# The first stage of an attention-and-mixing kernel: its loads further ahead and in program order, and two steps of token mixing exchanged

## The chip, the cores and the metric

The kernel runs on one core of a Trainium2 chip. The metric is the device time of one execution in microseconds (us). Three timed runs of the kernel before took 830.56, 832.79 and 835.46 us; the median is 832.79.

The engines carry the names of the profile: PE multiplies matrices (PEld loads its weights), DVE is the vector engine, ACT the scalar engine, POOL the GpSimd engine, and SP issues the transfers from memory (DMA). Each engine works through its own instructions in a fixed order, and so does SP with the transfers that it issues: an instruction that waits holds up all that stand behind it on the same engine.

## The reference

Three blocks follow each other. All matrices are float32 and the weights of the second block come as 64-bit floats.

```python
# 1. attention: 4 images, 8 heads, 576 positions, head width 64
#    a) pooled: q, k, v averaged over groups of 4 positions (144 groups), softmax, times v; each result serves 4 positions
#    b) local: only positions nearer than 4 to each other, softmax, times v
out = repeat(softmax(qd @ kd.T / 8) @ vd, 4) + softmax(mask(q @ k.T / 8)) @ v
# 2. mixing, x of 4 x 576 x 512
h  = relu(x.T @ w_tok1) @ w_tok2            # token mixing, 576 -> 256 -> 576
u  = x + h.T
y  = u + relu(u @ w_ch1) @ w_ch2            # channel mixing, 512 -> 1536 -> 512
# 3. four causal attention experts of width 64 with a gate that keeps the best two
```

## The kernel before

The program has three stages. The first holds the attention and the token mixing, the second the channel mixing, the third the experts. The change touches the first stage only, so this section stays with it.

A **unit** is one image and one pair of heads: 16 units, numbered 0 to 15. A unit's data are the queries `qT` (288 KB), the keys `kz` (two transfers of 144 KB, one for each head, into a tile whose other half is zero), the values by windows `vz` (two transfers of 160 KB) and the values for pooling `vp` (288 KB): 1,184 KB in all. The tiles `kz`, `vz` and `qz` exist `KB` and `VB` times and are used in turn; `KB` and `VB` are 3, and `vp` has two buffers.

The stage is a software pipeline. **Step i** of its loop (lines 468 to 486) does, for different units:

- `load_qk` asks for the queries and keys of unit i+3 (`LA` + 1);
- `values(i)` multiplies the finished probabilities with the values on PE: `pod` for the pooled part, `ol` for the local one. DVE adds both into `u`, the result. After it the tile `vz` of unit i is free;
- `local(i+2)` and `pooled(i+2)`: POOL and DVE form the pooled queries `qz` and keys `kd` (line 295, a sum over `kz` on DVE), PE forms the scores `sl` and `sd`, DVE their maxima (`nmx`, `nd`), ACT the exponentials (10 for `P`, 3 for `Pd`), DVE the reciprocals of the sums (`rs`, `rd`), POOL multiplies (lines 324 and 345);
- `turns(i+1)` transposes `P` and `Pd` on PE (`tl`, `pdt`), and ACT copies them to `PT` and `PdT`;
- `tok_step`, for a whole pair of units: `tok_turn` transposes `u` on PE (`tx`) and splits it into a high part on ACT (`xh`) and a low part on DVE (`xl`); `tok_first` multiplies with the first weights (`h`); `tok_second` with the second (`pu`, 24 products), and DVE adds to `u` (line 433). In even steps there are `tok_turn(i-2)` and `tok_second(i-4)`, in odd steps `tok_first(i-3)`;
- up to four of the seven pieces of token-mixing weights (`wt`) and, from step 3 on, one piece of the channel-mixing weights (`wc`, 512 KB each) are loaded and **converted**: two passes on ACT (lines 190, 192), three on DVE (194 to 196), one on POOL (200), and a split into high and low on ACT and DVE (137, 147);
- `load_v` asks for the values of unit i+3 (`VB`).

What sets the order: PE takes its instructions in the order of the program (`behind` ties each to the one before). For the other engines, and for SP, a scheduler in the compiler chooses the order by its own estimate of times, and moves loads and conversions ahead of the place where the program has them. So the distance at which a load is issued is not simply `LA` or `VB`. Products go to four PSUM banks of one kind and two pairs of another: a product waits until the bank that it gets has been read.

Of the kernel before, what the change touches and what calls it, by code (L numbers as in the profile page):

```python
# [7 lines left out]
F32 = mybir.dt.float32  # L8
# [8 lines left out]
B, H, S, D = 4, 8, 576, 64  # L17
# [9 lines left out]
PK, PQ = SD // 2, 2 * SD // 3  # L27
# [18 lines left out]
ZENG = ['any', 'any']  # L46
PRE = False
ABANKS, CBANKS = (4, 2), (6, 1)
START = 'q0 q1 v0 q2 v1 v2'
XLO = 'gpsimd'  # L50
CONV0 = 3
UB = 5
TAIL = [1, 1, 1, 1]
ULO = 'vector'
LA = 2
WT = 4
VB = 3
KB = 3


@with_exitstack
def body(ctx, tc, qT, kT, vw, vp, wt1, wt2, wc1, wc2, wq, wk, wvg, wo, out):
    nc = tc.nc

    def pool(name, side=None, space=None, stack=ctx):
        kw = {"side": side} if side else {}
        if space is not None:
            kw["space"] = space
        return stack.enter_context(tc.tile_pool(name=name, bufs=1, reuse_waits="tile", **kw))
# [21 lines left out]
    order = {"on": True, "last": None}  # L91

    def behind(ins):

        if order["on"]:
            if order["last"] is not None:
                tc.add_manual_dep(ins.ins, order["last"].ins.name,
                                  mybir.DependencyInfo(mybir.DependencyClass.NoSync, mybir.DependencyReason.DATA),
                                  reason="order")
            order["last"] = ins  # L100

    def mm(*a, **kw):
        behind(nc.tensor.matmul(*a, **kw))  # L103

    def tp(*a):
        behind(nc.tensor.transpose(*a))
# [29 lines left out]
    def split(hi, lo, src, relu=False, scale=None):  # L136
        nc.scalar.activation(hi, src, AF.Relu if relu else AF.Copy, **({"scale": scale} if scale else {}))  # L137
        lowpart(lo, src, hi, relu, scale)
# [18 lines left out]
    def flat(t, shape):  # L157
        return t.rearrange("p c n -> p (c n)") if len(shape) == 3 else t

    def load_split(p, dram, shape, name, stage):  # L160
        raw = stage.tile(shape, F32, tag="raw", bufs=2, name=name + "_raw")
        nc.sync.dma_start(raw, dram)
        hi = p.tile(shape, F32R, name=name + "_hi")
        lo = p.tile(shape, F32R, name=name + "_lo")
        split(hi, lo, raw)
        return hi, lo

    def load_f32(dram, shape, name, dst=None):

        P0, n = shape[0], 1  # L170
        for d in shape[1:]:
            n *= d
        if dram.dtype == F32:
            if dst is None:
                dst = pv.tile(shape, F32, tag="w64t", bufs=2, name=name + "_t")
            nc.sync.dma_start(dst, dram)
            return dst
        raw = pv.tile([P0, n, 2], I32, tag="raw64", bufs=2, name=name + "_raw")
        d32 = dram.bitcast(I32)
        if len(shape) == 3:  # L180
            nc.sync.dma_start(raw.rearrange("p (c n) t -> p c (n t)", c=shape[1]), d32)
        else:
            nc.sync.dma_start(raw.rearrange("p n t -> p (n t)"), d32)
        h = raw[:, :, 1]
        a = pv.tile([P0, n], I32, tag="w64a", bufs=2, name=name + "_a")
        f = pv.tile([P0, n], I32, tag="w64f", bufs=2, name=name + "_f")
        g = pv.tile([P0, n], F32, tag="w64g", bufs=2, name=name + "_g")
        t = pv.tile([P0, n], F32, tag="w64t", bufs=2, name=name + "_t")

        nc.scalar.activation(t.bitcast(I32), raw.bitcast(U32)[:, :, 0], AF.Copy, scale=2.0 ** -29)  # L190

        nc.scalar.activation(g, h.bitcast(F32), AF.Abs)

        nc.vector.tensor_scalar(a, h, 3, 0x3FFFFFF8, op0=OP.logical_shift_left, op1=OP.bitwise_and)
        nc.vector.scalar_tensor_tensor(f, h, -0x40000000, a, op0=OP.bitwise_and, op1=OP.bitwise_or)
        nc.vector.scalar_tensor_tensor(f.bitcast(F32), g, 2.0 ** -15, f.bitcast(F32), op0=OP.is_ge, op1=OP.mult)
        if dst is None:
            dst = t.rearrange("p (c n) -> p c n", c=shape[1]) if len(shape) == 3 else t

        nc.gpsimd.tensor_tensor(flat(dst, shape).bitcast(I32), f, t.bitcast(I32), op=OP.add)  # L200
        return dst
# [12 lines left out]
    pa = pool("pa", stack=sA)  # L214
# [27 lines left out]

    KZ = [pa.tile([128, 2, S], F32, name=f"kz{i}") for i in range(KB)]
    VZ = [pa.tile([128, 2, NW, D], F32, name=f"vz{i}") for i in range(VB)]

    QZ = [pa.tile([128, 2, SD], F32, name=f"qz{i}") for i in range(KB)]

    def zero(tiles, i, eng):

        for h in range(2):  # L250
            eng.memset(tiles[i][64 * h:64 * h + 64, 1 - h], 0.0)

    Vl, Vd = {}, {}

    def load_v(b, p):
        i = b * NP + p
        if i < VB:
            zero(VZ, i, getattr(nc, ZENG[1]))
        Vl[b, p] = VZ[(b * NP + p) % VB]
        for h in range(2):  # L260
            nc.sync.dma_start(Vl[b, p][64 * h:64 * h + 64, h], vw[b, p, 64 * h:64 * h + 64])
        raw = pa.tile([PK, 4, 4, D], F32, tag="vp", bufs=2, name=f"vp{b}{p}")
        nc.sync.dma_start(raw, vp[b, p])
        vd = pa.tile([PK, 4, D], F32, tag="vd", bufs=3, name=f"vd{b}{p}")
        spare("v", i).tensor_tensor(raw[:, :, 0:2], raw[:, :, 0:2], raw[:, :, 2:4], op=OP.add)
        spare("w", i).tensor_tensor(vd, raw[:, :, 0], raw[:, :, 1], op=OP.add)
        Vd[b, p] = vd
# [1 line left out]
    QK = {}  # L269

    def load_qk(b, p):
        q = pa.tile([128, S], F32, tag="qT", bufs=3, name=f"qT{b}_{p}")
        nc.sync.dma_start(q, qT[b, p])
        i = b * NP + p
        if i < KB:
            zero(KZ, i, getattr(nc, ZENG[0]))
            zero(QZ, i, nc.gpsimd)
        kz = KZ[i % KB]
        for h in range(2):
            nc.sync.dma_start(kz[64 * h:64 * h + 64, h], kT[b, p, 64 * h:64 * h + 64])  # L280
        QK[b, p] = (q, kz, QZ[i % KB])

    SC = {}
# [151 lines left out]
    units = [(b, p) for b in range(B) for p in range(NP)]  # L435
    for what in START.split():
        (load_qk if what[0] == "q" else load_v)(*units[int(what[1])])

    n = len(units)
# [20 lines left out]

    def tok_step(i):

        for what, k in ((tok_turn, i - 2), (tok_first, i - 3), (tok_second, i - 4)):
            if k % 2 == 0 and 0 <= k < n:
                with ahead(what.__name__):
                    what(units[k][0], units[k][1] // 2)

    for i in range(n):
        if i + LA + 1 < n:
            load_qk(*units[i + LA + 1])  # L470
        values(*units[i])
# [7 lines left out]
        tok_step(i)  # L479
        for _ in range(WT):  # L480
            if tokw:
                tokw.pop(0)()
        if i >= CONV0 and conv[0][0] == 0:
            convert()
        if i + VB < n:
            load_v(*units[i + VB])
    order["on"] = False
    sA.close()


# [279 lines left out]
    for i, (b, p) in enumerate(pairs):  # L770
# [13 lines left out]
        last = nxt is None  # L784
# [80 lines left out]
```

## Time and profile before

| | |
|---|---|
| median of three runs | 832.79 us |
| the profiled execution | 831.15 us |
| its span, first to last instruction | 829.3 us |
| PE busy in the span | 696.0 us (84%) |
| DVE, ACT, POOL busy | 492.0, 392.2, 163.4 us |
| TensorE clock granted, mean | 0.925 of full speed |
| DMA over the span | 57 GB/s |

The profiled execution lies 1.64 us under the median of the runs, and its span 1.85 us under its own time. The first stage ends at 277.5 us, where PE begins its first product of the channel mixing; from there to 560 us PE is almost never idle. The first 235 us are where PE stands still for much of the time, and a row of the timeline there shows in square brackets how long an engine was idle before an instruction and what ended that idle time.

### The profile page before, as it was taken

The numbers are of one execution on the slowest core, as the hardware profiler recorded it, in microseconds if no ns is written. First come the engines' busy times: TensorE is split into PE (matmuls) and PEld (weight loads), VectorE is DVE, ScalarE is ACT, GpSimd is POOL, SyncE is SP. The second block draws the span as 40 slices with busy tenths as digits, with TensorE's granted clock in tenths as the row PEclk, the third lists the DMA queues.
The fourth block names the chain that finished last, engine by engine and source line by source line (L and its number), as shares of the span: only waits on it lengthen the run. The fifth ranks groups of instructions, "written<-read, shape, count | busy, mean of one in ns | idle before, by whom it ended". The sixth has DMA issues, their size and how long they took to land. (4 is left out here: it accounts for less than half of the span.)

```text
span 829.3 us, 15409 instructions
## 1 busy us (share of the span) xinstructions
PE 696.0 (84%) x5816; PEld 648.7 (78%) x5816; DVE 492.0 (59%) x1203; ACT 392.2 (47%) x1273; POOL 163.4 (20%) x183
## 2 busy tenths in 40 slices
PE   4424468568589999999999999999989989989994
PEld 3324368557578999999999999999987868779863
DVE  5598955334445479487558445644287556657760
ACT  6356653363365254354344223422266475566662
POOL 5575653333321012020011000000420010010000
PEclk8567598798799999999999999999999999999997
DMA  8545552252210022031011001000021031021111
GB/s 208 141 126 171 157 123 60 60 117 60 59 34 2 1 89 65 2 116 37 1 51 53 1 1 39 15 1 1 1 58 31 1 86 30 9 78 30 44 45 57
DMA packets 28578, 46.88 MB, mean 57 GB/s; under 512 B 3224, under 2 KB 16024, under 8 KB 28504
## 3 DMA queue, kind: packets, MB, share of 16 engines
q1 hardware_dynamic: 28504, 45.90, 20.7%
q8 instruction: 46, 0.75, 0.4%
q14 instruction: 28, 0.23, 0.1%
HBM read 36.45 MB, written 4.72 MB: 50 GB/s over the span
## 5 line engine op out<-in xcount | busy, mean ns | idle before, releaser
L103 PE MATMUL c<-ul,wch 128*128 128x288 f32 x384 | 113.7, 296 | 0.6 <-DVE ul L506 0.6
L103 PE MATMUL c<-uh,wch 128*128 128x288 f32 x384 | 113.6, 296 | 0.4 <-DVE acc L529 0.4
L103 PE MATMUL c<-hh,wch 128*128 128x288 f32 x384 | 113.8, 296 | 0.0
L103 PE MATMUL c<-hh,wcl 128*128 128x288 f32 x384 | 113.2, 295 | 0.0
L103 PE MATMUL c<-hl,wch 128*128 128x288 f32 x384 | 113.2, 295 | 0.0
L103 PE MATMUL c<-uh,wcl 128*128 128x288 f32 x384 | 113.2, 295 | 0.0
L137 ACT ACTIVATE hh<-c 128x288 fp32r<-128x288 f32 x96 | 39.1, 408 | 122.1 <-PE c L103 122.1
L143 DVE SCALAR_TENSOR_TENSOR hl<-c,hh 128x288 fp32r<-128x288 f32 x96 | 43.5, 453 | 64.6 <-ACT hh L137 64.6
L103 PEld LDWEIGHTS c<-ul,wch 128*128 128x128 f32 x384 | 72.4, 189 | 1.5 <-DVE ul L506 1.3
L103 PEld LDWEIGHTS c<-uh,wch 128*128 128x128 f32 x384 | 72.2, 188 | 0.9 <-DVE acc L529 0.9
L103 PEld LDWEIGHTS c<-hh,wch 128*128 128x128 f32 x384 | 72.2, 188 | 0.2
L103 PEld LDWEIGHTS c<-hl,wch 128*128 128x128 f32 x384 | 72.3, 188 | 0.0
L103 PEld LDWEIGHTS c<-hh,wcl 128*128 128x128 f32 x384 | 72.3, 188 | 0.0
L103 PEld LDWEIGHTS c<-uh,wcl 128*128 128x128 f32 x384 | 72.2, 188 | 0.0
L200 POOL TENSOR_TENSOR wc_t<-wc_f,wc_t 128x512 int32<-128x512 int32 x24 | 33.7, 1409 | 171.3 <-ACT wc_t L190 155.3
L505 ACT ACTIVATE uh<-u 128x288 fp32r<-128x288 f32 x128 | 52.9, 441 | 27.3 <-PE c L103 27.3
L506 DVE TENSOR_TENSOR ul<-u,uh 128x288 fp32r<-128x288 f32 x128 | 56.4, 470 | 8.8 <-ACT uh L505 8.7
L700 ACT ACTIVATE Pc<-s,nm 112x576 f32<-112x576 f32 (+4 forms) x80 | 44.3, 555 | 25.6 <-DVE nm L697 13.2
L103 PE MATMUL pod<-PdT,vd 72*64 72x144 f32 x128 | 13.4, 339 | 50.7 <-ACT PdT L363 45.7
L103 PE MATMUL pu<-wt_hi,h1h 128*128 128x288 f32 x64 | 24.0, 375 | 36.4 <-DVE xl L147 35.2
L319 ACT ACTIVATE P<-sl,nmx 128x64 f32<-128x64 f32 x160 | 48.6, 341 | 8.7 <-DVE nmx L313 8.6
L295 DVE TENSOR_REDUCE kd<-kz 128x144 f32<-128x1152 f32 x16 | 21.6, 1348 | 51.3 <-DMA kz<-in_kT_dram 51.3
(166 smaller groups left out, 1880.1 us busy)
## 6 DMA issues: line engine op xcount, KB each, us to landing
wc_raw<-in_wc_dram SPq DMA_DIRECT2D x24, 512.0 KB
vz<-in_vw_dram SPq DMA_DIRECT2D x32, 160.0 KB
qT<-in_qT_dram SPq DMA_DIRECT2D x16, 288.0 KB
kz<-in_kT_dram SPq DMA_DIRECT2D x32, 144.0 KB
vp<-in_vp_dram SPq DMA_DIRECT2D x16, 288.0 KB
K<-K SPq DMA_DIRECT2D x64, 72.0 KB
out_dram<-y SPq DMA_DIRECT2D x16, 232.0 KB
wt_raw<-in_wt_dram SPq DMA_DIRECT2D x4, 288.0 KB
```

What stands on the lines that cost most here:

```text
L103: behind(nc.tensor.matmul(*a, **kw))
L137: nc.scalar.activation(hi, src, AF.Relu if relu else AF.Copy, **({"scale": scale} if scale else {}))
L143: nc.vector.scalar_tensor_tensor(lo, src, 0.0, h, op0=OP.max, op1=OP.subtract)
L200: nc.gpsimd.tensor_tensor(flat(dst, shape).bitcast(I32), f, t.bitcast(I32), op=OP.add)
L295: nc.vector.tensor_reduce(kd, kz.rearrange("p h (g r) -> p g h r", r=4), axis=AX.XY, op=OP.add)
L319: nc.scalar.activation(P[:, t, h], sv[:, bk, i], AF.Exp, bias=nmx[:, bk, i:i + 1], scale=0.125, accum_out=sm[:, t, h:h + 1])
L505: nc.scalar.activation(hi, u, AF.Copy)
L506: getattr(nc, ULO).tensor_tensor(lo, u, hi.bitcast(F32), op=OP.subtract)
L700: nc.scalar.activation(pv_, sv, AF.Exp, bias=nm[:nq], accum_out=su[:nq])
```

## The change

Six things are edited. `KB` and `VB` go from 3 to 4 and `vp` gets a third buffer (`vd` a fourth), so that `load_qk` asks for unit i+4 and `load_v` for unit i+4. The list of first loads `START` holds four units. All loads of the first stage go through a new helper `fetch`, which ties each load to the load before it, so that SP issues them in the order of the program, weights included. At most three pieces of `wt` go into a step. In `tok_step` the second product of token mixing now stands before the turning. The scratch memory that the compiler reserves for DMA descriptors is cut from 16 KB to 1 KB in each partition, which makes room for the larger tiles.

```diff
-START = 'q0 q1 v0 q2 v1 v2'
+START = 'q0 q1 v0 q2 v1 q3 v2 v3'
-LA = 2
-WT = 4
-VB = 3
-KB = 3
+LA = 3
+WT = 3
+VB = 4
+KB = 4
...
+    queue = {"on": True, "last": None}
+
+    def fetch(dst, src):
+
+        ins = nc.sync.dma_start(dst, src)
+        if queue["on"]:
+            if queue["last"] is not None:
+                tc.add_manual_dep(ins.ins, queue["last"].ins.name,
+                                  mybir.DependencyInfo(mybir.DependencyClass.NoSync, mybir.DependencyReason.DATA),
+                                  reason="queue")
+            queue["last"] = ins
...
-            nc.sync.dma_start(Vl[b, p][64 * h:64 * h + 64, h], vw[b, p, 64 * h:64 * h + 64])
-        raw = pa.tile([PK, 4, 4, D], F32, tag="vp", bufs=2, name=f"vp{b}{p}")
-        nc.sync.dma_start(raw, vp[b, p])
-        vd = pa.tile([PK, 4, D], F32, tag="vd", bufs=3, name=f"vd{b}{p}")
+            fetch(Vl[b, p][64 * h:64 * h + 64, h], vw[b, p, 64 * h:64 * h + 64])
+        raw = pa.tile([PK, 4, 4, D], F32, tag="vp", bufs=3, name=f"vp{b}{p}")
+        fetch(raw, vp[b, p])
+        vd = pa.tile([PK, 4, D], F32, tag="vd", bufs=VB, name=f"vd{b}{p}")
...
-        for what, k in ((tok_turn, i - 2), (tok_first, i - 3), (tok_second, i - 4)):
+        for what, k in ((tok_second, i - 4), (tok_turn, i - 2), (tok_first, i - 3)):
...
-    order["on"] = False
+    order["on"] = queue["on"] = False
...
-    nc = bacc.Bacc("TRN2", target_bir_lowering=False, num_devices=1)
+    nc = bacc.Bacc("TRN2", target_bir_lowering=False, num_devices=1, dynamic_dma_scratch_size=1024)
```

The other loads of the stage (`qT`, `kz`, `wt`, `wc`) change from `nc.sync.dma_start` to `fetch` in the same way.

**SP, the loads that are issued during step 6.** Before (`vp23` is unit 11, `vz0` will hold unit 9, `qT2_3` and `kz2` are unit 11):

```order
L263 DMA vp23_1878<-in_vp_dram 72x1024
L261 DMA vz0_111<-in_vw_dram 64x640 x2
L273 DMA qT2_3_1693<-in_qT_dram 128x576
L280 DMA kz2_110<-in_kT_dram 64x576 x2
L263 DMA vp30_2032<-in_vp_dram 72x1024
```

Now (`vz2` and `vp22` are unit 10, `qT2_3` and `kz3` unit 11, `wc2_1` a piece of the channel-mixing weights; all rows have the line of `fetch`):

```order
L106 DMA vz2_114<-in_vw_dram 64x640 x2
L106 DMA vp22_1540<-in_vp_dram 72x1024
L106 DMA qT2_3_1545<-in_qT_dram 128x576
L106 DMA kz3_111<-in_kT_dram 64x576 x2
L106 DMA wc2_1_raw_1692<-in_wc2_dram 128x1024
L106 DMA vz3_115<-in_vw_dram 64x640 x2
```

`vz` now leads the group in place of `vp`, the keys are those of the same unit 11 in both, and one piece of `wc` stands behind the keys of steps 2 to 8, where before all those pieces had been asked for by step 4.

**PE, step 6, from the turns of unit 7 to the values of unit 7.** Before:

```order
L106 MATMUL tx0_1447<-ident_58,u1_90 116x128 x4
L106 MATMUL tx1_1456<-ident_58,u1_90 116x128 x4
L106 MATMUL tx2_1465<-ident_58,u1_90 112x128 x2
L103 MATMUL pu_1472<-wt2_00_hi_475,h1h_1310 128x288
...
L103 MATMUL pu_1496<-wt2_11_hi_642,h1l_1311 128x288
L103 MATMUL pod_1529<-PdT_1438,vd13_1164 64x144 x4
```

Now:

```order
L118 MATMUL pdt_1459<-ident_58,Pd_1271 72x96 x6
L115 MATMUL pu_1467<-wt2_00_hi_614,h1h_1330 128x288
...
L115 MATMUL pu_1491<-wt2_11_hi_806,h1l_1331 128x288
L118 MATMUL tx0_1499<-ident_58,u1_90 116x128 x4
L118 MATMUL tx1_1508<-ident_58,u1_90 116x128 x4
L118 MATMUL tx2_1517<-ident_58,u1_90 112x128 x2
L115 MATMUL pod_1549<-PdT_1458,vd13_994 64x144 x4
```

The 24 products `pu` moved from behind the turning `tx` to ahead of it.

**DVE, the same step.** Before (`kd` is the pooled key of unit 11, `xl` the low part of the turned `u`, `rs` belongs to the softmax of unit 8):

```order
L295 TENSOR_REDUCE kd_1922<-kz2_110 128x144
L147 TENSOR_TENSOR xl_1453<-tx0_1447,xh_1452 116x512
L147 TENSOR_TENSOR xl_1462<-tx1_1456,xh_1461 116x512
L147 TENSOR_TENSOR xl_1469<-tx2_1465,xh_1468 112x256
L322 TENSOR_SCALAR rs_1408<-sm_1397 128x10
L323 RECIPROCAL rs_1408<-rs_1408 128x10
L433 TENSOR_TENSOR u0_89<-pu_1472,u0_89 128x288
```

Now:

```order
L445 TENSOR_TENSOR u0_89<-pu_1467,u0_89 128x288
L307 TENSOR_REDUCE kd_1942<-kz3_111 128x144
L445 TENSOR_TENSOR u0_89<-pu_1475,u0_89 128x288
L445 TENSOR_TENSOR u0_89<-pu_1483,u0_89 128x288
L206 TENSOR_SCALAR wc2_1_a_1694<-wc2_1_raw_1692 128x512
L445 TENSOR_TENSOR u0_89<-pu_1491,u0_89 128x288
L334 TENSOR_SCALAR rs_1428<-sm_1417 128x10
...
L159 TENSOR_TENSOR xl_1505<-tx0_1499,xh_1504 116x512
```

The sum `kd` of unit 11 still stands in step 6, now between the additions of token mixing; the first pass over a piece of `wc` stands ahead of `rs`, and `xl` comes last.

## Rows read from the trace of the kernel before

**Rows 1.** Busy time by stretch, cut at the starts of steps 0, 2, 5, 9, 12.
```profile
core 0: us, PE busy (x) PEld busy (x) DVE busy (x) ACT busy (x) POOL busy (x), PEclk, DMA share, GB/s
0.00:35.30 35.30, 10.85 (x81) 8.39 (x81) 16.37 (x32) 17.62 (x67) 17.40 (x41) 0.72 0.71 184
35.30:76.80 41.50, 15.21 (x188) 13.91 (x188) 37.51 (x55) 20.58 (x78) 27.45 (x27) 0.66 0.47 141
76.80:131.90 55.10, 34.29 (x355) 31.83 (x355) 42.48 (x72) 31.04 (x121) 31.41 (x30) 0.72 0.47 124
131.90:194.10 62.20, 40.90 (x503) 38.74 (x502) 25.10 (x60) 25.94 (x128) 22.45 (x28) 0.84 0.37 79
194.10:235.00 40.90, 29.40 (x375) 27.51 (x374) 16.22 (x40) 18.68 (x95) 12.90 (x16) 0.87 0.31 69
```

**Rows 2.** Waits from 131.86 to 235 us: total us, times, longest.
```profile
DVE kd L295 <- DMA kz<-in_kT_dram: 42.3, 6, 8.9
PE pu L103 <- DVE xl L147: 28.2, 3, 9.6
```

**Rows 3.** Timeline of SP in step 6: start, us, load issued.
```profile
146.75 0.33 SPq L263 DMA_DIRECT2D vp<-in_vp_dram  x1
...
149.00 1.10 SPq L280 DMA_DIRECT2D kz<-in_kT_dram  x2
```

**Rows 4.** Waits of SP over the whole span: total us, times, longest.
```profile
SPq L263 <- POOL vd L266: 89.5, 10, 14.5
```

**Rows 5.** Timeline of PE, steps 6 to 13; in brackets idle before and releaser.
```profile
141.85 0.71 PE L103 MATMUL pod<-PdT,vd 72*64 72x144 f32 x8 [1.13 <-ACT PdT L363]
142.40 1.33 PE L103 MATMUL ol<-PT,vz 128*64 128x58 f32 x40
...
157.83 0.61 PE L103 MATMUL pu<-wt_hi,h1h 128*128 128x288 f32 x1 [9.63 <-DVE xl L147]
...
163.10 0.71 PE L103 MATMUL pod<-PdT,vd 72*64 72x144 f32 x8
...
173.09 0.71 PE L103 MATMUL pod<-PdT,vd 72*64 72x144 f32 x8 [1.12 <-ACT PdT L363]
...
248.63 0.71 PE L103 MATMUL pod<-PdT,vd 72*64 72x144 f32 x8
```

**Rows 6.** Timeline of DVE in step 6, same columns.
```profile
155.83 1.35 DVE L295 TENSOR_REDUCE kd<-kz 128x144 f32<-128x1152 f32 x1 [8.92 <-DMA kz<-in_kT_dram]
157.10 1.61 DVE L147 TENSOR_TENSOR xl<-tx,xh 116x512 fp32r<-116x512 f32 x3
```

**Rows 7.** Groups of instructions to 268 us: busy us, mean ns, idle before.
```profile
L340 ACT ACTIVATE Pd<-sd,nd 96x144 f32<-96x144 f32 x48 | 18.1, 417 | 0.0
L147 DVE TENSOR_TENSOR xl<-tx,xh 116x512 fp32r<-116x512 f32 x14 | 9.1, 681 | 5.2 <-ACT xh L137 5.2
L137 ACT ACTIVATE xh<-tx 116x512 fp32r<-116x512 f32 x14 | 8.8, 634 | 0.0
L192 ACT ACTIVATE wc_g<-wc_raw 128x512 f32<-128x512 f32 x10 | 6.7, 685 | 9.3 <-DMA wc_raw<-in_wc_dram 9.3
```

**Rows 8.** Timeline of DVE before step 3: a key tile lands, pieces of `wc` land.
```profile
21.07 1.35 DVE L295 TENSOR_REDUCE kd<-kz 128x144 f32<-128x1152 f32 x1 [3.08 <-DMA kz<-in_kT_dram]
...
63.99 0.43 DVE L194 TENSOR_SCALAR wc_a<-wc_raw 128x512 int32<-128x512 int32 x1 [1.69 <-DMA wc_raw<-in_wc_dram]
...
66.86 0.43 DVE L194 TENSOR_SCALAR wc_a<-wc_raw 128x512 int32<-128x512 int32 x1 [0.32 <-DMA wc_raw<-in_wc_dram]
...
70.34 1.97 DVE L194 TENSOR_SCALAR wc_a<-wc_raw 128x512 int32<-128x512 int32 x1
```

**Rows 9.** Timeline of ACT before step 0.
```profile
33.47 0.67 ACT L190 ACTIVATE wt_t<-wt_raw 116x512 int32<-116x512 uint32 x1 [3.15 <-DMA wt_raw<-in_wt_dram]
...
34.59 0.63 ACT L363 ACTIVATE PdT<-pdt 72x576 f32<-72x576 f32 x1
```

**Rows 10.** Timeline of POOL, step 1.
```profile
69.10 2.93 POOL L200 TENSOR_TENSOR wc_t<-wc_f,wc_t 128x512 int32<-128x512 int32 x2
```

More of the change, by code (lines that the diff above doesn't have):

```diff
@@ L161, in load_split @@
         raw = stage.tile(shape, F32, tag="raw", bufs=2, name=name + "_raw")
-        nc.sync.dma_start(raw, dram)
+        fetch(raw, dram)
         hi = p.tile(shape, F32R, name=name + "_hi")
@@ L175, in load_f32 @@
                 dst = pv.tile(shape, F32, tag="w64t", bufs=2, name=name + "_t")
-            nc.sync.dma_start(dst, dram)
+            fetch(dst, dram)
             return dst
@@ L180, in load_f32 @@
         if len(shape) == 3:
-            nc.sync.dma_start(raw.rearrange("p (c n) t -> p c (n t)", c=shape[1]), d32)
+            fetch(raw.rearrange("p (c n) t -> p c (n t)", c=shape[1]), d32)
         else:
-            nc.sync.dma_start(raw.rearrange("p n t -> p (n t)"), d32)
+            fetch(raw.rearrange("p n t -> p (n t)"), d32)
         h = raw[:, :, 1]
@@ L271, in load_qk @@
     def load_qk(b, p):
-        q = pa.tile([128, S], F32, tag="qT", bufs=3, name=f"qT{b}_{p}")
-        nc.sync.dma_start(q, qT[b, p])
+        q = pa.tile([128, S], F32, tag="qT", bufs=KB, name=f"qT{b}_{p}")
+        fetch(q, qT[b, p])
         i = b * NP + p
@@ L279, in load_qk @@
         for h in range(2):
-            nc.sync.dma_start(kz[64 * h:64 * h + 64, h], kT[b, p, 64 * h:64 * h + 64])
+            fetch(kz[64 * h:64 * h + 64, h], kT[b, p, 64 * h:64 * h + 64])
         QK[b, p] = (q, kz, QZ[i % KB])
```

## Prediction

> **What bounds the kernel now.** I read the busy time by stretch first. PE is the engine with most to do, and the reader is to see where it stands still: in the five stretches up to 235 us it is busy for 130.7 us of 235 [rows 1]. No other engine is full there, except DVE between 35 and 77 us (37.5 of 41.5 us). So the first stage is bound by waits, and the list of waits comes next. From step 5 to step 12 two of them lead: DVE waits 42.3 us for keys, and PE waits 28.2 us, three times, until DVE has formed `xl` [rows 2]. The third view, the timeline of step 6, shows that these two are one chain. The step starts at 141.85 us (its `pod`), and its products with `vz` end at 143.73, 1.9 us later. SP issues the next group of loads only at 146.75, 4.9 us after the start, because `vp` leads the group and waits for a buffer that POOL frees with `vd` [rows 3, 4]. The keys, last in the group, are there at 155.83, 9.1 us after the first issue. DVE stands at `kd` until then; behind it come the three `xl`, and only the first of them frees the bank in which the products `pu` may begin, at 157.83 [rows 5, 6]. The 24 `pu` take until 163.1, and the step has lasted 21.25 us. The odd step behind it, which has neither `tx` nor `pu`, lasts 10.0 (163.10 to 173.09). All of the time from step 5 to 12 is pairs of this kind.
>
> **The change, part by part.** The sum is made in lengths of steps, against the profiled execution (831.15 us, 1.64 under the median).
>
> *Even steps without a weight (10).* SP's group is led by `vz` now, which waits only for the products of the step: first issue 2.0 us after the start in place of 4.9. The group is as large as before (1,184 KB), so I take the same 9.1 us: keys at 11.1, `kd` done at 12.4. The products `pu` no longer wait for `xl`; they run under the wait for the keys, 5.3 us that leave the chain. What is late next is the bank of `tx`: by the new order the second addition of token mixing, which frees it, stands behind `kd` on DVE, so `tx` begins at 12.4 + 0.5 (one addition, estimated a little under the 0.68 of `xl` [rows 7]) = 12.9. Then `tx`, the first `xh` (0.63) and `xl` (0.68) follow, some 14.6, and `ol` of the next step, which stands 0.55 us after that step's start, takes this bank. Length: about 14.1 us in place of 21. So the load itself comes only 2.9 us earlier, since `kd` of unit i+5 stands in step i in both orders; the greater part is the exchange in token mixing.
>
> *Odd steps without a weight (9, 11).* The 10.0 us there end with ACT's `PdT`, not with a load (PE waited 1.1 us for it [rows 5]). The keys now come at 11.1 and delay the softmax of the next turns by a few tenths: 10.3 each. Step 12 has no load any more; its `pu` no longer stand behind `xl`: 11.0 for 13.6 (235.00 to 248.63). Steps 9 to 12: 10.3 + 14.1 + 10.3 + 11.0 = 45.7 for 54.5 (194.1 to 248.6), **−8.8**.
>
> *Steps 2 to 8, with weights.* Here the change adds a wait. Program order puts one piece of `wc` behind the keys of each step, and DVE and ACT have its first passes ahead of `rs`, `xh` and, in three steps, `Pd`. Two pieces that were asked for together came 2.87 us apart [rows 8], so a piece lands 11.1 + 2.9 = 14.0 us after the start of its step. Queued behind it are, on ACT, two passes of 0.685 (15.4) and then `xh` or the three exponentials of `Pd` (about 1.1 with their overlap) [rows 7]. An even step then ends as above through `xh` and `xl`: 14.0 + 1.4 + 0.6 + 0.7 − 0.55 = 16.2. An odd one ends when `Pd`'s exponentials free the bank of the second `ol` (1.1 after a start): 14.0 + 1.4 + 1.1 − 1.1 = 15.4, and 14.7 in step 5, where one pass stands ahead. Step 2 gets 16.5 for a rest of `wt`. Steps 7 and 8 get four further pieces that the scheduler pulls forward, and the last of these waits for the buffer of the second before it with `vz` of unit 12 behind it on SP: I give both together 33. Sum: 16.5 + 15.4 + 16.2 + 14.7 + 16.2 + 33 = 112.0 for 117.3 (76.8 to 194.1), **−5.3**. This term is the least known. Its lower end is a weight that is there before it is needed: even steps 14.1, odd 10.2, seven steps 87, that is −30. Its upper end is a load group that takes 2.5 us longer with the piece in it in each step, 129.5, that is +12. I take the middle value since the rows of a weight's arrival and of ACT's passes are measured on this very tile.
>
> *Steps 0 and 1, and what lies ahead.* Before, `PdT` of unit 0 stood on ACT behind passes over a `wt` piece that landed at 33.47; step 0 began at 35.3 [rows 9]. In the new order ACT has `PdT` ahead of all `wt`. What holds it instead is `kd` of unit 3, now ahead of the first `rs`: 3,520 KB have to land before it, where 4,128 KB had landed at 21.07 [rows 8]. By that rate its keys land near 18.5 to 19; through `kd`, `rs`, POOL's `P` and `Pd` and PE's turns that gives 27.8: −7.5 (between −10, and −3 if the three further loads of the start are taken one after another). Steps 0 and 1 last 41.5 us in which DVE is 90% busy with conversions [rows 1]; two pieces of `wc` that stood ahead of step 1's maxima have moved on: −3.9, between −8 and 0. Together **−11.4**.
>
> *At nothing:* the zeroing of one more `kz`, `vz` and `qz`, which runs while the first keys are on the way; the scratch memory, since every load is issued from SP; steps 13 to 15 and all behind them, where no load of the units is left and the PE order of the second and third stage reads the same.
>
> Sum: −8.8 − 5.3 − 11.4 = −25.5 on 831.15, 805.6; with the 1.6 between this execution and the median, **807 us**.
>
> One rule is weighed here. DVE's first pass over a `wc` piece takes 0.43 us, but 1.97 at 70.34, while POOL was busy with `wc_t` until 72.03 [rows 8, 10]; beside such work a conversion's early passes cost up to 1.5 us more. The Trainium skill (SBUF — State Buffer, "Who interferes with whom") says that DVE and GpSimd share one pair of ports as a lock, the later one blocked for the other's whole instruction; by that rule, the trace agrees. One collision in each of seven steps would add up to 10 us to the sum; POOL is idle while the loads are awaited, so I add nothing.
>
> **The rivals.** *Weights hidden.* The pieces land early enough, so that steps 2 to 8 run at 14.1 and 10.2: 25 less, 782. For it: DMA is at 0.37 to 0.47 of its capacity in these stretches [rows 1]. Against it: the new order asks for the piece behind 1,184 KB that cannot be issued before the step's own products.
>
> *Small gain.* The exchange works as above, but a group with a weight takes 2.5 us longer than reckoned (112 becomes 129.5): 824. For it: all loads share one queue, and keys alone already take 9.1 us.
>
> *Slower by the queue's head.* `fetch` makes SP stop at a weight whose raw buffer (two of them) is still being converted, and behind it stand the values and keys of all units. If the piece lands 14.0 + 25.5/7 = 17.6 us after the start, the gain is used up; that is the point from which this decides. At 5 us for each of seven steps the time is 807 + 35 = 842. For it: SP already stood 89.5 us at the head of its queue [rows 4]. Against it: the buffer that a piece needs was emptied one step earlier, except in steps 7 and 8, which the sum has.
>
> *Not what it says.* The loads are not really further ahead: `vz` waits for `values(i)` as before and DVE takes the same unit's keys. This is in the sum already; that the exchange of `pu` gives nothing either would leave −11 for the start and −12 for the earlier issue less the +12 of weights: about 822, in the small gain.
>
> **How the numbers follow.** Forecast 807, with its own range 797 to 817: 0.58. Weights hidden (775 to 797): 0.15. Small gain (817 to 828): 0.16. Queue's head, no gain or slower: 0.11. A measurement of this kernel tells about 0.5% (4 us) from no change, so faster means under 828.6: 0.58 + 0.15 + 0.15 = 0.88; within 0.5% 0.06, slower 0.06. The range from 786 to 826 leaves out about 0.06 below and 0.13 above.
>
> **What would show it.** In the profile after: the idle time of PE before `pu` gone, and before `tx` or `ol` of the odd step some 5 us instead; even steps from 6 to 10 of 14 to 16 us; SP's first issue of a group 2 us after a step's start, and the keys 9 us later; DVE still idle before `kd`, for shorter; ACT's largest idle ended by `wc`; step 0 near 28, step 9 near 177, channel mixing from about 252 in place of 277.5, and the same length behind it. Wrong would be shown by `wc` landing over 17 us after its step's start, or by a stretch behind 277 us that changed its length.

## The result

The changed kernel takes 803.28 us (median of four runs, 800.97 to 804.44); the kernel before, run beside it, 831.99. The ratio is 0.9646, with a 95% interval from 0.9607 to 0.9684. The profiled execution took 802.79 us (before 831.15), its span 801.0 (829.3). Channel mixing begins at 249.33 us, before at 277.49, and what lies behind that point has the same length (551.7 and 551.8 us). So all of the 28 us is in the first stage.

Cut at the same steps as [rows 1], which now start at 28.69, 67.63, 112.53, 171.94 and 208.97 us, the busy time by stretch of the kernel after (us; busy time and instructions of each engine; granted clock; DMA share; GB/s) is:

```profile
0.00:28.69 28.69, 9.59 (x79) 7.80 (x79) 14.40 (x26) 16.37 (x65) 18.21 (x44) 0.80 0.82 197
28.69:67.63 38.94, 16.57 (x187) 14.68 (x187) 21.78 (x48) 18.89 (x74) 20.00 (x24) 0.63 0.46 119
67.63:112.53 44.90, 31.19 (x354) 29.15 (x354) 25.21 (x57) 25.46 (x112) 20.24 (x24) 0.80 0.45 118
112.53:171.94 59.41, 42.88 (x501) 39.30 (x501) 41.22 (x84) 35.88 (x146) 32.37 (x32) 0.91 0.55 145
171.94:208.97 37.03, 31.43 (x374) 29.02 (x375) 19.91 (x49) 19.03 (x97) 17.83 (x22) 0.91 0.32 84
```

PE's busy time in each stretch is within 3.1 us of what it was; the stretches are shorter by 6.6, 2.6, 10.2, 2.8 and 3.9 us. DVE's work has moved: 21.8 us for 37.5 in steps 0 and 1, 41.2 for 25.1 in steps 5 to 8, because the pieces of `wc`, which DVE began to convert between 64 and 107 us, are now begun one by one from 81 to 172 us, from the end of step 2 to the end of step 8.

The waits of steps 5 to 11 (total us, times, longest) show what became of the two that led before, 42.3 us at `kd` and 28.2 at `pu` [rows 2]:

```profile
DVE kd L307 <- DMA kz<-in_kT_dram: 19.5, 6, 4.7
...
PE tx L118 <- DVE u L445: 5.5, 2, 4.3
ACT wc_t L202 <- DMA wc_raw<-in_wc_dram: 4.8, 3, 2.2
```

The wait before `pu` is gone. Step 6 on PE (start, us, tile, idle time before and its releaser) is now:

```profile
123.82 0.71 PE L115 MATMUL pod<-PdT,vd 72*64 72x144 f32 x8 [0.87 <-ACT PdT L375]
...
127.07 1.54 PE L115 MATMUL ol<-PT,vz 128*64 128x58 f32 x24 [2.08 <-ACT Pd L352]
...
132.52 0.38 PE L115 MATMUL pu<-wt_hi,h1h 128*128 128x288 f32 x1
...
140.25 2.35 PE L118 MATMUL tx<-ident,u 128*116 128x128 f32 x10 [4.31 <-DVE u L445]
142.53 0.99 PE L115 MATMUL pod<-PdT,vd 72*64 72x144 f32 x6
```

The `pu` start as soon as the products before them are through, and `tx` waits for an addition into `u`, 4.3 us. That addition stands on DVE behind `kd`, and `kd` waits for the keys:

```profile
138.48 1.35 DVE L307 TENSOR_REDUCE kd<-kz 128x144 f32<-128x1152 f32 x1 [4.43 <-DMA kz<-in_kT_dram]
139.75 0.81 DVE L445 TENSOR_TENSOR u<-pu,u 128x288 f32<-128x288 f32 x2
```

The wait for keys is still there; 9.6 us of idle time before 24 products have become 4.3 before 10 transposes.

### The profile page after: what moved, and what is told of

Same layout as the page of the kernel before. It is cut to its first block, busy times and chain, and to the rows that moved or that the text cites. A ratio compares the mean times of both kernels' runs of the same rounds, so it can differ in the third digit from the quotient of the medians.

```text
span 801.0 us, 15367 instructions
## 1 busy us (share of the span) xinstructions
PE 695.3 (87%) x5816; PEld 646.5 (81%) x5816; DVE 477.3 (60%) x1205; ACT 393.9 (49%) x1275; POOL 160.3 (20%) x185
## 3 DMA queue, kind: packets, MB, share of 16 engines
q1 hardware_dynamic: 28504, 45.90, 21.4%
## 5 line engine op out<-in xcount | busy, mean ns | idle before, releaser
L517 ACT ACTIVATE uh<-u 128x288 fp32r<-128x288 f32 x128 | 52.9, 441 | 27.5 <-PE c L115 27.5
L331 ACT ACTIVATE P<-sl,nmx 128x64 f32<-128x64 f32 x160 | 47.5, 333 | 35.1 <-DVE nmx L325 30.2
L709 DVE TENSOR_REDUCE nm<-s 112x1 f32<-112x576 f32 (+4 forms) x80 | 40.5, 514 | 8.7 <-PE s L705 7.6
L621 POOL TENSOR_TENSOR vlo<-u,vh 128x576 fp32r<-128x576 f32 x16 | 22.7, 1444 | 93.1 <-ACT vh L620 93.1
```

The lines of the kernel that those rows point to most:

```text
L331: nc.scalar.activation(P[:, t, h], sv[:, bk, i], AF.Exp, bias=nmx[:, bk, i:i + 1], scale=0.125, accum_out=sm[:, t, h:h + 1])
L517: nc.scalar.activation(hi, u, AF.Copy)
L621: getattr(nc, XLO).tensor_tensor(lo, U[b][:, c], hi.bitcast(F32), op=OP.subtract)
L709: nc.vector.tensor_reduce(nm[:nq], sv, axis=AX.X if t < 4 else AX.XY, op=OP.max, negate=True)
```

## The experiments

Each run was timed beside the kernel before, with three rounds, and its ratio to that kernel is given. The stage table shows where a run won or lost; it is read from the `pod` starts of the profiled executions (us).

| | to step 0 | steps 0–1 | 2–4 | 5–8 | 9–12 | 13 to channel mixing | channel mixing begins |
|---|---|---|---|---|---|---|---|
| before | 35.3 | 41.5 | 55.1 | 62.2 | 54.6 | 28.9 | 277.5 |
| after | 28.7 | 38.9 | 44.9 | 59.4 | 48.7 | 28.7 | 249.3 |
| exchange only | 36.1 | 41.4 | 52.3 | 58.0 | 51.8 | 28.7 | 268.3 |
| after, no exchange | 27.4 | 37.8 | 48.3 | 66.5 | 49.9 | 28.8 | 258.7 |
| after, no tie | 29.1 | 49.0 | 52.8 | 45.1 | 43.0 | 29.2 | 248.2 |
| buffers only | 27.5 | 48.8 | 51.0 | 40.7 | 43.9 | 28.9 | 240.8 |
| values' buffers only | 38.7 | 40.6 | 57.9 | 60.2 | 48.4 | 28.9 | 274.7 |
| after, `kd` late | 29.1 | 38.6 | 44.6 | 59.8 | 47.9 | 29.5 | 249.5 |
| after, pieces late | 27.4 | 38.8 | 39.9 | 49.8 | 64.1 | 33.5 | 253.5 |
| pieces and `kd` late | 27.5 | 38.6 | 33.6 | 45.1 | 60.6 | 32.0 | 237.4 |
| and `vd` late | 29.7 | 39.5 | 35.1 | 43.9 | 67.1 | 31.5 | 246.8 |
| after, keys before values | 28.5 | 40.2 | 46.0 | 59.1 | 43.8 | 28.9 | 246.5 |
| the same, no exchange | 28.9 | 39.4 | 48.7 | 66.3 | 43.9 | 28.8 | 256.0 |
| pieces, `kd` late, rest held | 27.3 | 38.6 | 34.0 | 43.7 | 58.0 | 32.0 | 233.6 |

### Taking the change apart: exchange, buffers, tie

The change has three parts: the exchange in `tok_step`; the buffers with `START`, `LA` and `WT`; and the tie that puts SP's loads in program order (`fetch`). Four runs split them.

**Exchange only**, on the kernel before:

```diff
-        for what, k in ((tok_turn, i - 2), (tok_first, i - 3), (tok_second, i - 4)):
+        for what, k in ((tok_second, i - 4), (tok_turn, i - 2), (tok_first, i - 3)):
```

> The kernel before with one edit: the second product of token mixing stands before its turning; loads, buffers and weights as before. Theory A (the exchange takes the wait for the keys off the chain): the keys still come 14.0 us after a step's start, but only tx (one addition and 1.2 us of transposes) stands behind them, so an even step without a weight lasts about 17.0 for 21 us (three of them, -12) and step 12 some -2.6; 813 to 819 us. Theory B (the gain comes from the loads and the weights' order): at most -5, 827 to 832 us.

Measured: 822.74 us, 0.9884 (0.9851 to 0.9917). That is 8.6 us less than the kernel before, between the ranges of the two theories. Steps 6, 8 and 10 last 18.1, 18.9 and 17.2 us for 21.2, 21.0 and 20.9, so the mechanism is there, at 2 to 4 us a step; `tx` waits 6.9 us in step 6 where `pu` had waited 9.6:

```profile
155.90 2.38 PE L106 MATMUL tx<-ident,u 128*116 128x128 f32 x10 [6.87 <-DVE u L433]
```

Step 12 won only 0.4.

**After without the exchange**, the rest as changed:

```diff
-        for what, k in ((tok_second, i - 4), (tok_turn, i - 2), (tok_first, i - 3)):
+        for what, k in ((tok_turn, i - 2), (tok_first, i - 3), (tok_second, i - 4)):
```

> The changed kernel with the old order of token mixing (turning, first, second product); buffers, START and program order of the loads as changed. Theory A: kd is done 12.4 us after an even step's start, then xl, then the 5.3 us of pu: some 18.6 us for each even step in place of 14 to 16, the start and steps 0 to 1 stay improved; 812 to 820 us. Theory B: within 4 us of the changed kernel, 799 to 807.

Measured: 815.94 us, 0.9803 (0.9759 to 0.9848): theory A. In the changed kernel the exchange is worth 12.6 us by the medians. The loss lies in steps 4, 6 and 8 (21.4, 21.7, 24.9 us for 17.3, 18.7, 18.1); the profiled execution, the fastest of the four, begins channel mixing 9.4 us later than the changed kernel.

**After without the tie**, SP's order left to the scheduler:

```diff
-    queue = {"on": True, "last": None}
+    queue = {"on": False, "last": None}
```

> The changed kernel without the tie between loads: the scheduler chooses SP's order, with four buffers for keys and values, three for vp and the exchange. It puts vp ahead of vz again and bunches the weights early. Theory C (program order of the loads matters by itself): steps 0 to 5 lose again what was won, about 812 to 822 us. Rival (buffers and exchange do all): 799 to 807 us.

Measured: 799.57 us, 0.9606 (0.9552 to 0.9660), not to be told from the changed kernel, and in the rival's range. But the order of the loads does matter by stages. Steps 0 to 4 lose 18 us, as theory C has it: the scheduler again asks for ten pieces of `wc` early, and DVE begins to convert them in steps 1 to 3. Steps 5 to 12 win 20: step 6 lasts 11.1 us for 18.7.

**Buffers only**, the changed kernel with neither tie nor exchange:

```diff
-    queue = {"on": True, "last": None}
+    queue = {"on": False, "last": None}
...
-        for what, k in ((tok_second, i - 4), (tok_turn, i - 2), (tok_first, i - 3)):
+        for what, k in ((tok_turn, i - 2), (tok_first, i - 3), (tok_second, i - 4)):
```

> The changed kernel without the tie between loads and without the exchange: what is left is START, four buffers for keys and values, three for vp, LA and WT. Theory A2 (buffers pay only together with the exchange, since pu stands behind kd): only the start's 6 to 8 us, 820 to 826 us, and the exchange on top of it is worth over 20. Rival (the buffers give the larger part by themselves, as in the run with the tie and without the exchange): 810 to 818.

Measured: 793.10 us, 0.9533 (0.9517 to 0.9549), 10 us *less* than the changed kernel and below the ranges of both theories. So the idea that the buffers need the exchange falls. By the busy times of steps 5 to 8 (columns as above) PE is busy there for 37.4 of 40.7 us, at the full clock:

```profile
127.30:168.00 40.70, 37.39 (x501) 35.30 (x500) 28.73 (x60) 26.14 (x129) 23.18 (x30) 1.00 0.51 121
```

The scheduler lets SP ask for queries and keys of unit i+6 in step i; the tie has those of unit i+5 there. In the timeline of SP, the keys of unit 11 are asked for in step 5:

```profile
131.63 1.11 SPq L106 DMA_DIRECT2D kz<-in_kT_dram  x2
```

DVE's timeline has their sum in step 6, 10.4 us later, with no idle time before it:

```profile
142.07 1.34 DVE L307 TENSOR_REDUCE kd<-kz 128x144 f32<-128x1152 f32 x1
```

With these runs one way from the kernel before to the kernel after has parts of different sign: 832 → 793.1 by the buffers (−39), → 815.9 by the tie (+23), → 803.3 by the exchange (−13). What a part is worth depends on the others: with the exchange put in first, the parts are −9 (exchange), −23 (buffers) and +4 (tie, within the noise). The tie on its own, without the buffers, was not run. Without the exchange, the tie wins 11 us in steps 0 and 1 and 3 in steps 2 to 4, and loses 26 and 6 in steps 5 to 8 and 9 to 12. And the exchange is worth something only where keys are waited for: without the tie it *costs* 6.5 us by the medians (799.6 for 793.1; the intervals just miss each other). Why it costs there was not followed up.

**Values' buffers only**, on the kernel before: which buffers are it?

```diff
-START = 'q0 q1 v0 q2 v1 v2'
+START = 'q0 q1 v0 q2 v1 v2 v3'
...
-VB = 3
+VB = 4
...
-        raw = pa.tile([PK, 4, 4, D], F32, tag="vp", bufs=2, name=f"vp{b}{p}")
+        raw = pa.tile([PK, 4, 4, D], F32, tag="vp", bufs=3, name=f"vp{b}{p}")
...
-        vd = pa.tile([PK, 4, D], F32, tag="vd", bufs=3, name=f"vd{b}{p}")
+        vd = pa.tile([PK, 4, D], F32, tag="vd", bufs=VB, name=f"vd{b}{p}")
...
-    nc = bacc.Bacc("TRN2", target_bir_lowering=False, num_devices=1)
+    nc = bacc.Bacc("TRN2", target_bir_lowering=False, num_devices=1, dynamic_dma_scratch_size=1024)
```

> The kernel before with a fourth buffer for the values, a third for vp, a fourth for vd and v3 in START (and the scratch memory that makes room for them); keys, queries, their order, the exchange and the tie as before. Theory K (the fourth buffer of the keys lets them be asked for a unit earlier, and that is the gain of 39 us of the run with all buffers): the keys stay behind vz, at most 2 to 4 us for each even step from 4 on, 815 to 826 us. Theory V (vp, which led the group and waited for vd, was the whole wait): 793 to 805 us.

Measured: 829.11 us, 0.9961 (0.9946 to 0.9977), a smaller gain still than theory K allowed. DVE still waits 31.3 us for keys from step 5 to 11. So `vp` at the head of SP's group was not the wait that counted. What the run with all buffers has beyond this one is the fourth buffer of the keys and queries (of `kz`, `qz` and also `qT`), with `LA`, `WT` and the fourth unit in `START`; nearly all of the 39 us need these. They were not run without the values' buffers, nor one by one.

### What holds the steps under the tie

**Pieces late**: the six `wc` pieces of the first stage in steps 9 to 14.

```diff
-CONV0 = 3
+CONV0 = 9
```

> The changed kernel with the six wc pieces of the first stage in steps 9 to 14 in place of 3 to 8 (CONV0 = 9). Theory E (a ring governs steps 2 to 8: group of loads, the piece behind it, ACT's two passes, xh or Pd, ol, then the next group, 13.5 to 15 us for each turn): without the piece these steps go toward 10.3 and 14.1, about 88 for 104 us, and steps 9 to 14, whose PE is nearly full, give back some 3 to 8: 788 to 798 us. Rival F (the piece is hidden by the keys' wait): 800 to 806. Rival G (pieces come too late for the channel mixing): over 806.

Measured: 807.95 us, 0.9732 (0.9694 to 0.9770), in the range of rival G, but not for its reason: what lies behind the start of channel mixing takes no longer (550.2 us for 551.7). Steps 2 to 8 fall from 104.3 to 89.7 us, as theory E has it, but ten pieces (these six, and four of the second group that follow them in either kernel) cost 20 us from step 9 on (64.1 for 48.7, then 33.5 for 28.7), not 3 to 8. DVE's wait for keys is unchanged in steps 2 to 8 (27.7 us; 26.6 in the changed kernel).

**`kd` late**, one buffer for it, so that DVE takes keys that were asked for two steps earlier:

```diff
-        kd = pa.tile([128, SD], F32, tag="kd", bufs=3, name="kd")
+        kd = pa.tile([128, SD], F32, tag="kd", bufs=1, name="kd")
```

> The changed kernel with one buffer for kd in place of three: DVE sums the keys of unit i+3 in step i in place of those of unit i+5, which are being loaded. Theory D (what still holds the even steps is DVE standing at kd): DVE's 46 us of waits for keys go, tx and ol stop waiting, steps 6, 8, 10 fall from 18.7, 18.1, 15.0 to 14 or less; 788 to 796 us. Rival (the transfers themselves bound the steps, and the wait shows up at vp or wc): 800 to 806 us.

Measured: 799.11 us, 0.9597 (0.9559 to 0.9635). That is 0.9 us under the rival's range and not to be told from the changed kernel; what happens is what the rival says. DVE's waits for keys are gone (0.5 us in all), but in their place DVE now stands at the piece behind them; steps 2 to 8 last 104.4 us, as in the changed kernel. From the waits of these steps (total us, times, longest):

```profile
DVE wc_a L206 <- DMA wc_raw<-in_wc_dram: 22.9, 7, 4.9
```

**Pieces and `kd` late**, both edits:

```diff
-CONV0 = 3
+CONV0 = 9
-        kd = pa.tile([128, SD], F32, tag="kd", bufs=3, name="kd")
+        kd = pa.tile([128, SD], F32, tag="kd", bufs=1, name="kd")
```

> As the run with the pieces in steps 9 to 14, and one buffer for kd, so that DVE sums keys that were asked for two steps earlier. Theory D (with the pieces gone, DVE's wait for keys is what holds tx and ol in steps 2 to 9): even steps fall to 11 to 12 us, 776 to 788 us. Rival (loads bound the steps, and the wait shows up elsewhere): within 3 us of the run without this edit.

Measured: 791.32 us, 0.9515 (0.9495 to 0.9535), 3 us over the range of theory D and far from its rival's. Steps 2 to 8 last 78.7 us, and PE is busy for 68 of them. So two arrivals hold these steps, one behind the other: without the piece they fall from 104.3 to 89.7 us, without the keys' wait as well to 78.7, and taking the keys' wait alone gives nothing. (Moving a piece takes away its transfer, its conversion and the wait for it together; the runs don't tell these apart.) The price is at steps 9 to 12, which last 60.6 us for 48.7. The busy times of steps 2 to 8 and 9 to 12 show DVE nearly as full as PE in the second:

```profile
66.10:144.80 78.70, 68.05 (x855) 62.99 (x855) 49.83 (x105) 47.68 (x233) 39.75 (x50) 0.93 0.45 116
144.80:205.40 60.60, 47.07 (x501) 42.28 (x500) 45.81 (x91) 38.00 (x150) 29.86 (x27) 0.84 0.42 121
```

**And `vd` late**, so that POOL doesn't stand at `vp` early:

```diff
-        vd = pa.tile([PK, 4, D], F32, tag="vd", bufs=VB, name=f"vd{b}{p}")
-        spare("v", i).tensor_tensor(raw[:, :, 0:2], raw[:, :, 0:2], raw[:, :, 2:4], op=OP.add)
-        spare("w", i).tensor_tensor(vd, raw[:, :, 0], raw[:, :, 1], op=OP.add)
+        vd = pa.tile([PK, 4, D], F32, tag="vd", bufs=2, name=f"vd{b}{p}")
+        v2 = pa.tile([PK, 4, 2, D], F32, tag="v2", bufs=1, name=f"v2{b}{p}")
+        spare("v", i).tensor_tensor(v2, raw[:, :, 0:2], raw[:, :, 2:4], op=OP.add)
+        spare("w", i).tensor_tensor(vd, v2[:, :, 0], v2[:, :, 1], op=OP.add)
```

> As the run with late pieces and late kd, and the pooled values vd formed about two units later as well (one intermediate tile, two buffers for vd), so that POOL doesn't stand at vp (58 us in the changed kernel) with P and Pd behind it. Theory H (POOL's wait at vp delays P and Pd, and these the turns): 3 to 8 us faster than the run without this edit. Rival (POOL's wait lies beside other work): within 3 us of it.

Measured: 799.50 us, 0.9618 (0.9587 to 0.9649), 8 us more. POOL no longer waits for `vp` in steps 9 to 12, but for queries (9.3 us), and PE for `PdT` (7.5 us). The gain of theory H did not come, and the rival's "within 3 us" did not hold either. Since the later order brought waits of its own, this run can't tell whether POOL's wait at `vp` held the turns. Why it costs 8 us was not followed up.

**Keys before values**, tie kept: the loads of queries and keys one unit further ahead, in front of the next values.

```diff
+    load_qk(*units[KB])
     for i in range(n):
-        if i + LA + 1 < n:
-            load_qk(*units[i + LA + 1])
         values(*units[i])
...
+        if i + KB + 1 < n:
+            load_qk(*units[i + KB + 1])
         if i + VB < n:
             load_v(*units[i + VB])
```

> The changed kernel, tie and exchange kept, with one block moved: the loads of a unit's queries and keys stand in the program ahead of the next values' load, not behind it, one unit further ahead (unit i+5, whose buffer is free since the step before), with the step's weight piece in front of them. Theory K (the tie's price is that the keys of unit i+5 stand behind a vz that waits for values(i), while DVE sums these same keys in step i): keys and piece land before they are needed, DVE's 46 us of waits for keys fall under 15, steps 3 to 10 fall to 9 to 13 us, and the spread weights keep steps 0 to 2 short; 778 to 790 us. Rival (the transfers' or engines' own time bounds these steps): 797 to 806.

Measured: 799.34 us, 0.9607 (0.9572 to 0.9643): the rival's range, and not to be told from the changed kernel. Steps 9 to 12, without pieces, fall from 48.7 to 43.8 us, what the kernel with the buffers only has (43.9): there, the keys' place behind `vz` was the tie's price. The wait for keys over the first stage falls from 46 us, as theory K has it:

```profile
DVE kd L307 <- DMA kz<-in_kT_dram: 10.9, 5, 4.5
```

But steps 2 to 8 take 105.1 us: by their waits DVE stands at the piece again.

```profile
DVE wc_a L206 <- DMA wc_raw<-in_wc_dram: 17.0, 8, 5.7
```

**The same without the exchange**, this edit on the run before:

```diff
-        for what, k in ((tok_second, i - 4), (tok_turn, i - 2), (tok_first, i - 3)):
+        for what, k in ((tok_turn, i - 2), (tok_first, i - 3), (tok_second, i - 4)):
```

> As the run with the keys ahead of the values, with the old order of token mixing. Theory K: once the keys are there in time, the exchange is worth nothing or costs the 6 us that it cost without the tie: 772 to 786 us, 0 to 8 below the run with the exchange. Rival (the exchange always pays under a tie, as its 12.6 us in the changed kernel): 8 to 14 above it.

Measured: 808.61 us, 0.9716 (0.9686 to 0.9747), 9.3 us above the run before: the rival. Steps 9 to 12 are alike (43.9), so there the exchange is indeed worth nothing, as theory K has it; in steps 2 to 8, where the piece is waited for, it is worth 10 us (115.0 for 105.1). So here it pays where DVE stands at a late arrival in an even step, be it keys or a piece.

**Pieces and `kd` late, the second group's pieces held**, built on the run with both late. A load that stands in the program behind the first stage is placed behind that stage's last product in the scheduler's order:

```diff
+        elif not order["on"]:
+            tc.add_manual_dep(ins.ins, order["last"].ins.name,
+                              mybir.DependencyInfo(mybir.DependencyClass.NoSync, mybir.DependencyReason.DATA),
+                              reason="hold")
```

> As the run with the wc pieces from step 9 on and late kd, and in addition the loads of all further pieces (those of the second group, four of which stood converted in steps 12 and 13, where step 12 lasted 20.0 us with DVE busy without a break) are held behind the last product of the first stage. Theory W (a piece costs some 2.3 us of the first stage wherever DVE and ACT convert it, and nothing in the channel mixing, where PE is the bound): steps 12 and 13 fall from 33.7 to some 25, 781 to 785 us. Rival (the four pieces fill idle time): 788 to 794 us. Against both: the second group comes too late for the channel mixing, over 794.

Measured: 788.67 us, 0.9493 (0.9440 to 0.9545), in the rival's range. By the medians it is the fastest of all, 15 us under the changed kernel, but its interval covers that of the run that it is built on. Steps 12 and 13 fell to 30.1 us for 33.7, not to 25; channel mixing begins 3.8 us earlier, and from there on the program takes 0.8 us longer. So the four pieces, whose conversions begin between 226 and 237 us now, cost about 1 us each in steps 12 and 13 (one execution of each kernel), and theory W's 2.3 is too much. Three pieces of the first group still come close together, between 181 and 188 us, where step 12 begins at 184 and lasts 17.5 us; spreading these was not tried.

## Why the prediction was right, and where it was not

Predicted 807 us, own range 797 to 817; measured 803.3. The terms against the profiled executions (us):

| term | predicted | measured |
|---|---|---|
| start to step 0 | −7.5 | −6.6 |
| steps 0 and 1 | −3.9 | −2.6 |
| steps 2 to 8 | −5.3 | −13.0 |
| steps 9 to 12 | −8.8 | −5.9 |
| step 13 and behind | 0 | −0.3 |

The number is in part luck: the largest error, 7.7 us too little gain in steps 2 to 8, stands against 5.1 us too much in the three other terms.

**Start and steps 0, 1.** Near what was reckoned: `kd` of unit 3 begins at 19.84 us (18.5 to 19 predicted; the rate that the prediction names gives 18.0), step 0 at 28.7 (27.8).

**The exchange.** Right as a mechanism: `pu` left the chain, `tx` waits in its place, behind `kd` and an addition, and two runs put its price at 8.6 us (kernel before) and 12.6 us (changed kernel). The 5.3 us for the `pu`, which the prediction took off the chain, were long in part by the clock: the 24 `pu` of step 6 take 3.4 us now. Before, they followed 9.6 us of idle time. The busy times of just this stretch of the kernel before, in which the granted clock is 0.60:

```profile
157.80:163.10 5.30, 5.27 (x24) 5.10 (x25) 3.11 (x9) 0.00 (x0) 2.17 (x2) 0.60 0.00 0
```

And of the kernel after, at 1.00:

```profile
132.50:135.90 3.40, 3.40 (x27) 3.20 (x25) 1.06 (x4) 3.40 (x21) 1.07 (x1) 1.00 1.05 243
```

At 0.60 PE is mostly at the lower of its levels (1.2 GHz of 2.4). What now stands behind the idle time is `tx`, 2.35 us where it took 1.26 before; the granted clock is 0.53 in its stretch:

```profile
140.20:142.50 2.30, 2.25 (x10) 1.94 (x10) 2.26 (x9) 1.62 (x4) 0.27 (x1) 0.53 0.00 0
```

**Steps 9 to 12.** Predicted 45.7, measured 48.7. A group's keys are there 8.9 us after its first issue (175.54 to 184.41; 9.1 predicted). What failed is that SP's first issue comes 2.0 us after a step's start: it came after 3.6 and 4.4 us in steps 9 and 10. In step 10 the second part of `ol` itself waits 2.3 us for ACT's `Pd`, and `vz` waits for `ol`:

```profile
187.10 0.91 PE L115 MATMUL ol<-PT,vz 128*64 128x58 f32 x24 [2.31 <-ACT Pd L352]
```

```profile
188.04 1.11 SPq L106 DMA_DIRECT2D vz<-in_vw_dram  x2
```

**Steps 2 to 8.** The mis-sized term. The prediction had the piece at 14.0 us after a step's start: 2.0 to the first issue, 9.1 to the keys, 2.9 more to the piece. In steps 3 to 6 it came after 13.1, 15.4, 12.8 and 15.9, on average 14.3, but by other parts, as the turn from step 3 to step 4 shows. On ACT the passes over the piece and the exponentials of `Pd` behind them, and the first pass over the next piece:

```profile
97.14 0.67 ACT L202 ACTIVATE wc_t<-wc_raw 128x512 int32<-128x512 uint32 x1 [2.06 <-DMA wc_raw<-in_wc_dram]
97.71 0.66 ACT L204 ACTIVATE wc_g<-wc_raw 128x512 f32<-128x512 f32 x1
98.27 0.36 ACT L352 ACTIVATE Pd<-sd,nd 96x144 f32<-96x144 f32 x1
...
110.64 0.67 ACT L202 ACTIVATE wc_t<-wc_raw 128x512 int32<-128x512 uint32 x1 [0.68 <-DMA wc_raw<-in_wc_dram]
```

On PE the second part of `ol`, which needs the bank that these exponentials read:

```profile
99.50 0.80 PE L115 MATMUL ol<-PT,vz 128*64 128x58 f32 x10 [3.14 <-ACT Pd L352]
```

On SP the first load of the group, which waits for `ol`, and the next piece at the group's end:

```profile
101.06 1.10 SPq L106 DMA_DIRECT2D vz<-in_vw_dram  x2
...
104.42 0.52 SPq L106 DMA_DIRECT2D wc_raw<-in_wc_dram  x1
```

And on DVE the sum of the group's keys:

```profile
109.52 1.35 DVE L307 TENSOR_REDUCE kd<-kz 128x144 f32<-128x1152 f32 x1 [2.91 <-DMA kz<-in_kT_dram]
```

The piece lands 9.6 us after the group's first issue, 1.1 us behind the keys, not 2.9. At the rate of the group, 1,184 KB in 8.5 us, its 512 KB would take 3.7 us by themselves (an estimate), so most of them came beside the group; the two pieces of [rows 8], one behind the other, were the wrong row. The first issue, in turn, comes 5.9 us after the start of step 4, since the products that free `vz` wait for ACT behind the previous piece. It is a ring: piece, two passes, `Pd` (or `xh` and `xl`), `ol`, group, next piece. Its turn is 13.5 us here, 14.6 and 14.4 for the next two. Steps 3 and 4 last 28.4 us together (31.6 predicted), 5 and 6 30.0 (30.9), 7 and 8 29.4 (33): the 7.7 us by which the term was off. The runs agree with the ring: with the pieces late these steps fall by 14.6 us, and with the keys' wait taken away alone they stay.

**Signs that did not come.** Of what the prediction named to look for, SP's first issue came 2.6 to 5.9 us after a step's start in steps 3 to 10, not 2; steps 6 and 8 lasted 18.7 and 18.1 us, not 14 to 16; and ACT's largest idle time in steps 0 to 15 was ended by DVE's `nmx` (22.4 us), not by `wc` (10.4).

**The rivals.** "Weights hidden" is excluded: the piece was waited for in these steps, which last 104.3 us and not 87. "Small gain" is excluded too: a group with a piece did not take 2.5 us longer, its keys came 8.3 to 9.9 us after its first issue in steps 3 to 8, around the 9.1 of before. "Slower by the queue's head" needed a piece 17.6 us after its step's start; in steps 3 to 6 the latest came after 15.9. SP did stand at the pieces' buffers in step 7, where four pieces took it 10.5 us to issue; the sum had that in the 33 us for steps 7 and 8, which lasted 29.4. "Not what it says" was taken as in the sum, and for the tied program it holds.

What the prediction did not see is what the loads would do untied. It named the exchange the greater part of an even step's gain; against the tie it is worth 13 us, alone 9, and without the tie it costs 6.5. The buffers by themselves, 39 us, and what the tie takes back, 23, stand in no term of the prediction. Of the scratch memory, taken at nothing, no run splits off the time: every run with a fourth buffer has it cut.

**What stays open:** the cost of a piece in steps 9 to 13 (1 us by the last run, 2 by the run with pieces late), which of the added buffers the 39 us need, and whether the fastest version would gain without its tie.

## What to carry to other kernels

A tie that puts loads into program order also fixes which load stands behind which wait: before adding it, read for each load what the one in front of it waits for, and compare with the order that the scheduler chose. Where two late arrivals stand one behind the other on one engine, taking one away shows nothing: take both away in a third run. And try the parts of a change in all combinations when one can cover another's loss: here the exchange repaired a part of what the tie had broken, and the buffers by themselves were faster than the whole.

## Not expected of the hardware

Two things. The exchange is in part an exchange of what PE does right behind a long wait: 24 products at 0.60 of the clock or 10 transposes at 0.53 (above), 1.9 us lost on the one and 1.1 on the other.

And a short operation on DVE can last many times its length beside POOL. In the run with pieces and `kd` late, DVE's scaling of `nd`, 96 x 3 elements, took 0.15 us and then 1.24:

```profile
184.63 0.15 DVE L348 TENSOR_SCALAR nd<-nd 96x3 f32<-96x3 f32 x1
...
200.96 1.24 DVE L348 TENSOR_SCALAR nd<-nd 96x3 f32<-96x3 f32 x1
```

POOL's `wc_t` stood beside the second one, and itself took 2.35 us for 1.26 at 174.84:

```profile
174.84 1.26 POOL L212 TENSOR_TENSOR wc_t<-wc_f,wc_t 128x512 int32<-128x512 int32 x1
...
199.83 2.35 POOL L212 TENSOR_TENSOR wc_t<-wc_f,wc_t 128x512 int32<-128x512 int32 x1 [4.43 <-DVE wc_f L208]
```

Both end at 202.2. The rule that the prediction weighed (the Trainium skill, SBUF — State Buffer, "Who interferes with whom") has the later of the two blocked for the other's instruction; here the trace agrees: DVE operations of 0.41, 0.16 and 0.68 us ran to 201.0 while POOL's operation grew by 1.09 us, and then the scaling of `nd` grew by 1.09 beside POOL. So the length lost is set by the neighbour's operation, not by that of the blocked one.

The prediction added nothing for it, since POOL would be idle while loads are awaited. In the changed kernel that held for the most part: of DVE's first and second passes over ten pieces two were long, a first one of 2.27 us at 161.2 and a second one of 1.66 at 156.8, for some 0.42 and 0.69 elsewhere, both beside an operation of POOL. A collision can also cost more than the 1.5 us that it took from [rows 8]: at 81.49 in the kernel before, a first pass took 2.44 us. In step 12 of the run above, where conversions crowd, DVE was busy for 19.5 of 20.0 us, and such time is part of it.
